# Sliding-window attention followed by SoLU and a layer norm, on one core: the division by the softmax sum is left out, and another search sets the order

## The chip, the core and the metric

One NeuronCore of a Trainium2 chip runs the whole program. Its engines work through queues of their own and meet at semaphores: PE (TensorE, matmuls; PEld is its weight load), DVE (VectorE), ACT (ScalarE), POOL (GpSimd) and SP (SyncE, which here only issues DMAs). The metric is the device time of one execution, in microseconds. The median of three runs of the kernel before is 397.25 us (396.76 to 397.73).

## The reference

Attention over a window of 31 keys and over 24 summaries of key blocks, then a two-layer network whose activation is a SoLU with a layer norm. Batch 4, 8 heads, 768 positions, 64 values a head; the network has 3072 tokens, 512 inputs and 1024 hidden values. All of it is float32.

```python
def _attn_ref(q, k, v):
    k_sum = k.reshape(B, H, nb, block, D).max(axis=3)     # block 32, nb 24
    v_sum = v.reshape(B, H, nb, block, D).mean(axis=3)
    scores_l = scale * np.matmul(q, k.transpose(0, 1, 3, 2))
    mask_l = np.abs(pos[:, None] - pos[None, :]) < window   # 16
    scores_s = scale * np.einsum('bhsd,bhnd->bhsn', q, k_sum) + np.log(block)
    scores_all = np.concatenate([np.where(mask_l, scores_l, -1e9), scores_s], axis=-1)
    ...
    a = a / (np.sum(a, axis=-1, keepdims=True) + 1e-09)
    return np.matmul(a, np.concatenate([v, v_sum], axis=2))

def _moe_ref(x, w_in, w_out, g_ln):
    h = x @ w_in
    e = np.exp(h - np.max(h, axis=-1, keepdims=True))
    sm = e / (np.sum(e, axis=-1, keepdims=True) + 1e-9)
    solu = h * sm
    mu = np.mean(solu, axis=-1, keepdims=True)
    var = np.mean((solu - mu) ** 2, axis=-1, keepdims=True)
    ln = (solu - mu) / np.sqrt(var + 1e-06) * g_ln
    return ln @ w_out
```

The layer norm takes the scale of its input out again. With Z the softmax sum, solu is u / Z for u = h * e, and (solu - mu) / sqrt(var + 1e-6) equals (u - mean(u)) / sqrt(var(u) + 1e-6 * Z * Z).

## The kernel before

The attention goes by steps: a batch, a group of four 64-query blocks (three groups a batch), and half of the heads. A step makes scores (L578, tile s), masks them and takes their minima on DVE (L597), exponentiates on ACT (L605), divides by the sum (L288), turns the result over on PE (L633, tile t), copies it out (at), and multiplies it with the values (L672, tile x; vt holds a group's value windows and, in its last 24 rows, the block means). x is split into a rounded part xh and a rest xl, since float32 matmuls are made of three matmuls of rounded parts. Two steps fill the inputs of two tiles of 128 tokens.

The network goes by those 24 tiles. `first(t)` makes h in two halves of 512 (L697, 12 matmuls each), takes the maxima (L707), exponentiates with the sum kept in hz (L712), adds the two halves' sums and takes the reciprocal on DVE (L715, L718), multiplies h by the exponential and the reciprocal with the row sum kept (L720), subtracts the mean (L723; L728, L730 or L732 on POOL, DVE or ACT), squares (L735), and makes y, the inverse root, on POOL (L739 to L745: a power by -0.5 and a step of refinement). `turn(t)` turns the tile over (lt) and splits it into lh and ll (L760); `second(t)`, four tiles behind, multiplies with w_out (L775, tile o) and scales by y on the way out (L780, os). A tile's h halves lie in PSUM banks that a later tile's h waits for (three banks for the first three tiles, then two), so L720 is also what frees a bank.

The two weight matrices come in 16 pieces of 128x1024 words. Each is rebuilt and rounded in several passes (L368 to L402, tiles raw, cv, w) on ACT, DVE and POOL, before the first matmul that reads it. `LOADS` lists the order of the first loads on SP: w a piece of w_in, k a pair of heads' keys, q queries, r rows of values for the block means of the first batch (L447, tile st_v), v value windows; capitals are the next group's.

The order is not written by hand. Every operation goes into `Plan.op` with the engines that can do it, a cost in us, and what it reads and writes. `Plan.order` plays the program: each engine takes the ready operation that can start first, and among equals that with the lowest due number. `Plan.issue` did this 64 times with noise of 3.0 on the due numbers, each time on the original numbers, and kept the order whose last matmul ended first. `keep_up` fills PE's expected pauses up to 80 us with matmuls on zeros (L900, "fillers"), which are part of the program: once queued, they are done. The plan counts a DMA's landing as 0.6 us behind its transfer up to 50 us and as 2.0 behind that.

The means of the first two batches are made on PE from loaded rows (L459, and L472 for the second batch); a DMA copies them into the last rows of each group's vt (L541, "vt<-vsum"). Those of the first batch's groups after the first went through ACT's queue, all later ones through SP's. The second batch's means go through ACT and four small DMAs on its queue (L483, L485).

## Time and profile before

| | before |
|---|---|
| median of 3 runs | 397.25 us |
| the profiled execution | 397.45 us, of which the span is 395.7 |
| PE busy, matmul instructions recorded | 386.6 us, 3697 |
| DVE, ACT, POOL busy | 275.4, 248.7, 97.9 us |
| fillers (L900), weight loads recorded | 83 |
| HBM read, written | 40.11 MB, 6.29 MB |

The page gives the busy time of each engine over the whole span, the queries give it for stretches of the span, and the rows of the timeline give single instructions with their start, their length, and in brackets how long the engine stood idle ahead of them and what ended that. A few per cent of the matmul records are missing, so counts from the order of the program are used where a count matters. The granted clock was 1.00 in every stretch up to the last matmul.

### The profile page before, as it was taken

The numbers are of one execution on the slowest core, as the hardware profiler recorded it, in microseconds if no ns is written. First come the engines' busy times: TensorE is split into PE (matmuls) and PEld (weight loads), VectorE is DVE, ScalarE is ACT, GpSimd is POOL, SyncE is SP. The second block draws the span as 40 slices with busy tenths as digits, with TensorE's granted clock in tenths as the row PEclk, the third lists the DMA queues.
The fourth block names the chain that finished last, engine by engine and source line by source line (L and its number), as shares of the span: only waits on it lengthen the run. The fifth ranks groups of instructions, "written<-read, shape, count | busy, mean of one in ns | idle before, by whom it ended". The sixth has DMA issues, their size and how long they took to land.

```text
span 395.7 us, 9677 instructions
## 1 busy us (share of the span) xinstructions
PE 386.6 (98%) x3697; PEld 298.3 (75%) x3703; DVE 275.4 (70%) x884; ACT 248.7 (63%) x746; POOL 97.9 (25%) x245
## 2 busy tenths in 40 slices
PE   8999998999999999999999999999999999999996
PEld 3436766677878888878888888878888887878776
DVE  4999998999789866577767657657657654554330
ACT  3889686999798756658558466468466463533411
POOL 4224010416837221236220121221021021101100
PEclk9999999999999999999999999999999999999999
DMA  7999992136277320463330410430310000000011
GB/s 287 411 410 369 409 329 78 56 113 185 70 248 208 113 103 0 141 175 104 123 112 2 150 66 27 156 73 28 108 48 27 2 28 27 16 12 28 27 55 53
DMA packets 14994, 49.24 MB, mean 124 GB/s; under 512 B 1836, under 2 KB 2092, under 8 KB 13412
## 3 DMA queue, kind: packets, MB, share of 16 engines
q1 hardware_dynamic: 11084, 41.89, 30.8%
q10 hardware_dynamic: 3864, 6.74, 4.7%
q8 instruction: 29, 0.48, 0.5%
q14 instruction: 17, 0.14, 0.1%
HBM read 40.11 MB, written 6.29 MB: 117 GB/s over the span
## 4 chain that ended last, share of the span: by engine, by line
PE 85%; DMA 6%; ACT 3%; DVE 2%; issue 1%; ACTq 1%; SPq 1%; DVEq 0%
PE o L775 35%; PE h L697 30%; PE x L672 6%; PE s L578 5%; PE t L633 3%; PE lt L633 3%; DMA st_v<-in_vr 3%; DMA raw<-in_w_in 2%; DMA vt<-vsum 2%; PE vs_ps L459 1%; PE x L900 1%; ACT he L712 1%; DVE he L720 1%; ACT at L281 1%; PE x L664 1%
## 5 line engine op out<-in xcount | busy, mean ns | idle before, releaser
L775 PE MATMUL o<-w,lh 128*128 128x512 f32 (+1 forms) x400 | 128.0, 390 | 0.1
L697 PE MATMUL h<-w,xh 128*128 128x512 f32 x384 | 127.0, 398 | 0.4 <-DVE he L720 0.4
L605 ACT ACTIVATE e<-e,nm 128x120 f32<-128x120 f32 x192 | 73.1, 385 | 25.0 <-DVE nm L597 25.0
L775 PEld LDWEIGHTS o<-w,lh 128*128 128x128 f32 x400 | 74.1, 188 | 18.5 <-issue 2.4
L697 PEld LDWEIGHTS h<-w,xh 128*128 128x128 f32 x384 | 72.1, 188 | 18.9 <-ACT e L605 0.8
L775 PE MATMUL o<-w,ll 128*128 128x512 f32 (+1 forms) x200 | 76.9, 384 | 0.0
L697 PE MATMUL h<-w,xl 128*128 128x512 f32 x192 | 75.6, 394 | 0.0
L707 DVE TENSOR_REDUCE hm<-h 128x1 f32<-128x512 f32 x48 | 32.6, 686 | 42.7 <-PE h L697 42.7
L281 ACT COPY at<-t 120x512 f32<-120x512 f32 x46 | 24.8, 587 | 46.1 <-PE t L633 45.6
L775 PEld LDWEIGHTS o<-w,ll 128*128 128x128 f32 x200 | 37.6, 188 | 6.6
L697 PEld LDWEIGHTS h<-w,xl 128*128 128x128 f32 x192 | 36.1, 188 | 7.5
L597 DVE CUSTOM_DVE_ANT_0 e<-s,mask 128x120 f32<-128x120 f32 x192 | 40.6, 276 | 1.3 <-PE s L578 1.3
L712 ACT ACTIVATE he<-h,hm 128x512 f32<-128x512 f32 x48 | 32.8, 697 | 9.4 <-DVE hm L709 9.4
L605 ACT ACTIVATION_READ_ACCUMULATOR e<-e,nm 128x1 f32 x192 | 36.5, 190 | 0.0
L760 DVE TENSOR_TENSOR ll<-lt,lh 128x512 fp32r<-128x512 f32 x48 | 31.9, 682 | 6.0 <-ACT lh L281 5.8
L739 POOL TENSOR_SCALAR ss<-ss 128x1 f32<-128x1 f32 x24 | 7.1, 297 | 115.0 <-ACT sq L735 114.9
L720 DVE SCALAR_TENSOR_TENSOR he<-h,hz,he 128x512 f32<-128x512 f32 x48 | 34.1, 746 | 0.4
L672 PE MATMUL x<-at,vt 120*64 120x64 f32 (+1 forms) x768 | 28.3, 225 | 1.5 <-ACT at L281 1.5
L672 PEld LDWEIGHTS x<-at,vt 120*64 120x64 f32 (+1 forms) x768 | 24.6, 138 | 6.3 <-ACT at L281 2.8
L288 DVE TENSOR_TENSOR e<-e,z 128x960 f32<-128x960 f32 x23 | 26.6, 1156 | 0.5
L281 ACT CAST lh<-lt 128x512 fp32r<-128x512 f32 x33 | 18.6, 596 | 12.9 <-PE lt L633 10.0
L735 ACT ACTIVATE sq<-he 128x1024 bf16<-128x1024 f32 x24 | 25.2, 1050 | 0.2
(94 smaller groups left out, 499.6 us busy)
## 6 DMA issues: line engine op xcount, KB each, us to landing
vt<-in_v SPq DMA_DIRECT2D x12, 1024.0 KB, 5.4
kraw<-in_k SPq DMA_DIRECT2D x16, 400.0 KB, 9.1
out<-os ACTq DMA_DIRECT2D x23, 256.0 KB, 2.0
qt<-in_q SPq DMA_DIRECT2D x11, 512.0 KB, 5.5
raw<-in_w_in SPq DMA_DIRECT2D x8, 512.0 KB, 10.7
raw<-in_w_out SPq DMA_DIRECT2D x8, 512.0 KB, 9.5
st_v<-in_vr SPq DMA_DIRECT2D x6, 512.0 KB, 12.5
st_v<-in_vb SPq DMA_DIRECT2D x8, 384.0 KB, 3.3
```

Source lines behind the costliest of these rows:

```text
L281: by = {act: lambda: nc.scalar.copy(out=to(), in_=of()), dve: lambda: nc.vector.tensor_copy(out=to(), in_=of()), pool: lambda: nc.gpsimd.t ...
L288: by = {dve: lambda: nc.vector.tensor_tensor(out=to(), in0=a(), in1=b(), op=kind), pool: lambda: nc.gpsimd.tensor_tensor(out=to(), in0=a() ...
L597: nc.vector.tensor_tensor_reduce(out=e.ap[:, n, :], in0=sc.ap[:, j, (2 * i + up) * KC:(2 * i + up + 1) * KC], in1=mask[:, mi, :], scale=-S ...
L605: nc.scalar.activation(out=e.ap[:, n, :], in_=e.ap[:, n, :], func=AF.Exp, bias=nm.ap[:, n:n + 1], scale=-1.0, accum_out=z.ap[:, n:n + 1])
L672: nc.tensor.matmul(xp()[j * D:(j + 1) * D, i, qs], vs.ap[:k, u, cs], at.ap[:k, u % 2, n[j] + u // 2, :], start=not apart, stop=not apart o ...
L697: nc.tensor.matmul(hp.ap, a.ap[:, c, ts], w.ap[:, i], start=(c == 0 and n == 0), stop=(c == NKC - 1 and n == 2))
L707: op(dve, 0.6, lambda i=i, hp=hp: nc.vector.tensor_reduce(out=nms.ap[:, i:i + 1], in_=hp.ap, op=ALU.max, axis=AX.X, negate=True), r=[hp], ...
L712: op(act, 0.71, lambda i=i, hp=hp: nc.scalar.activation(out=part(i), in_=hp.ap, func=AF.Exp, bias=nm.ap, accum_out=zs.ap[:, i:i + 1]), r=[ ...
L720: op(dve, 0.67, lambda i=i, hp=hp: nc.vector.scalar_tensor_tensor(out=part(i), in0=hp.ap, scalar=zs.ap[:, 0:1], in1=part(i), op0=ALU.mult, ...
L735: op(act, 1.13, lambda: nc.scalar.activation(out=sq.ap, in_=e.ap, func=AF.Square, accum_out=ss.ap), r=[e], w=[sq, ss])
L760: op(dve, 0.6, lambda part=part, r=r: nc.vector.tensor_tensor(out=part(lo), in0=tp.ap[:, r], in1=part(hi).bitcast(F32), op=ALU.subtract), ...
L775: nc.tensor.matmul(o.ap[:, cols], a.ap[:, f, :], w.ap[:, i, cols], start=(f == 0 and n == 0), stop=(f == NFC - 1 and n == 2))
```

## The change

The SoLU's division is left out: L720's product has 1.0 in place of the reciprocal, and the sum and the reciprocal (L715, L718 on DVE) are gone. Three operations of one element on POOL form (Z + 1e-9), times 1e-3, squared, and L739's addition takes that in place of the constant 1e-6. In the attention one broadcast of the first batch's means (its third group's) goes through SP instead of ACT. The planner's numbers and its search are others: 800 tries with a noise of 10, the first 16 on the original numbers, later ones on the best so far with noise on 2% of the operations; each order is then replayed six times with other durations and later landings (`replay`), and the sum of the last matmul's end and half of the mean end decides. `LOADS` has another order.

```diff
-LOADS = "wwkwqkkkqwwwrrrwwvQV"
+LOADS = "wkwqkkwkqwwrwrrwwvQV"
...
-    LATE = 50.0
+    LATE = 30.0
...
-    TRIES, NOISE = 64, 3.0
+    TRIES, NOISE = 800, 10.0
+    FIRST, FEW = 16, 0.02
+    PLAYS, JITTER, LAND = 6, 0.06, 1.5
...
-        due, best = [o.due for o in self.ops], None
-        for seed in range(self.TRIES):
-            noise = random.Random(seed)
-            for o, x in zip(self.ops, due):
-                o.due = x + (noise.gauss(0.0, self.NOISE) if seed else 0.0)
+        due, best, rnd = [o.due for o in self.ops], None, random.Random(0)
+        for i in range(self.TRIES):
+            noise = [x + (rnd.gauss(0.0, self.NOISE) if i < self.FIRST or rnd.random() < self.FEW else 0.0) * (i > 0)
+                     for x in (best[3] if i >= self.FIRST else [0.0] * len(due))]
+            for o, x, n in zip(self.ops, due, noise):
+                o.due = x + n
             order = self.order()
             if order:
-                end = max(o.end for o in order if "pe" in o.can)
-                if best is None or end < best[0]:
+                end = sum(self.replay(order, random.Random(k)) for k in range(self.PLAYS))
+                if best is None or end <= best[0]:
...
+    def replay(self, order, rnd):
+        free, end, held, dma, last, total, n = {}, {}, 0.0, 0.0, 0.0, 0.0, 0
+        for o in order:
+            e = o.engine
+            t = max([free.get(e, self.START)] + [end[d] + (0.0 if d.engine == e == "pe" else self.SYNC) for d in o.deps])
+            x = o.can[e][0] * (1 if e == "pe" else 1.0 + self.JITTER * (rnd.random() - 0.2))
+            other = free.get("pool", 0.0) if e == "dve" and o.port else held if e == "pool" else 0.0
+            x = t + x * (2 if e == "pe" and t < self.COLD else 1) + max(other - t, 0.0)
+            free[e] = end[o] = x
+            if e == "dve" and o.port:
+                held = x
+            if o.nbytes:
+                dma = max(dma, x + 1.0) + o.nbytes / (self.RATE if dma > self.COLD else self.SLOW) * 1e-3
+                end[o] = dma + (0.6 if dma < self.LATE else 2.5) + rnd.expovariate(1.0) * self.LAND * (dma > self.LATE)
+            if e == "pe":
+                last, total, n = max(last, x), total + x, n + 1
+        return last + 0.5 * total / n
...
-                o.end = dma + (0.6 if dma < self.LATE else 2.0)
+                o.end = dma + (0.6 if dma < self.LATE else 2.5)
...
-        e, cost, queue = (sp, 0.43, nc.sync) if b else (act, 0.8, nc.scalar)
+        e, cost, queue = (sp, 0.43, nc.sync) if b or g > 1 else (act, 0.8, nc.scalar)
...
-        op(dve, 0.07, lambda: nc.vector.tensor_scalar(
-            out=zs.ap[:, 0:1], in0=zs.ap[:, 0:1], scalar1=zs.ap[:, 1:2], scalar2=1e-9, op0=ALU.add, op1=ALU.add),
-           w=[zs])
-        op(dve, 0.1, lambda: nc.vector.reciprocal(out=zs.ap[:, 0:1], in_=zs.ap[:, 0:1]), w=[zs])
+        op(pool, 0.3, lambda: nc.gpsimd.tensor_tensor(
+            out=zs.ap[:, 0:1], in0=zs.ap[:, 0:1], in1=zs.ap[:, 1:2], op=ALU.add), w=[zs])
+        op(pool, 0.3, lambda: nc.gpsimd.tensor_scalar(
+            out=zs.ap[:, 0:1], in0=zs.ap[:, 0:1], scalar1=1e-9, scalar2=1e-3, op0=ALU.add, op1=ALU.mult), w=[zs])
+        op(pool, 0.3, lambda: nc.gpsimd.tensor_tensor(
+            out=zs.ap[:, 0:1], in0=zs.ap[:, 0:1], in1=zs.ap[:, 0:1], op=ALU.mult), w=[zs])
         for i, hp in enumerate(hs):
             op(dve, 0.67, lambda i=i, hp=hp: nc.vector.scalar_tensor_tensor(
-                out=part(i), in0=hp.ap, scalar=zs.ap[:, 0:1], in1=part(i), op0=ALU.mult, op1=ALU.mult,
-                accum_out=ss1.ap[:, i:i + 1]), r=[hp, zs], w=[(e, i), (ss1, i)])
+                out=part(i), in0=hp.ap, scalar=1.0, in1=part(i), op0=ALU.mult, op1=ALU.mult,
+                accum_out=ss1.ap[:, i:i + 1]), r=[hp], w=[(e, i), (ss1, i)])
...
-            out=ss.ap, in0=ss.ap, scalar1=1.0 / DF, scalar2=1e-6, op0=ALU.mult, op1=ALU.add), w=[ss])
+            out=ss.ap, in0=ss.ap, scalar1=1.0 / DF, scalar2=zs.ap[:, 0:1], op0=ALU.mult, op1=ALU.add), r=[zs], w=[ss])
```

The whole order moves, and with it the lines: what was L697 is L722, L720 is L749, L541 is L566, L900 is L929. Three places of it follow; each row is a line, an operation, what it writes and what it reads. In the new order PE has 31, 15, 2, 8, 3, 5 and 4 fillers ahead of its first h matmul (before: 19, 5, 17, 12, 8, 4 and 7), with both head halves' first scores in one piece each, and 3, 1, 7 and 2 behind it (before: 1, 7 and 3).

SP, the start of its queue, up to the first rows of values that PE reads for the means (st_v_0). Before, from its first row:

```order
L356 DMA raw_93<-in_w_in 128x1024
L430 DMA kraw_0_99<-in_k 128x800
L529 DMA qt_0_101<-in_q 128x512 x2
L430 DMA kraw_0_99<-in_k 128x800
L356 DMA raw_105<-in_w_in 128x1024
L356 DMA raw_107<-in_w_in 128x1024
L356 DMA raw_109<-in_w_in 128x1024
L430 DMA kraw_1_111<-in_k 128x800 x2
L356 DMA raw_117<-in_w_in 128x1024
L356 DMA raw_119<-in_w_in 128x1024
L529 DMA qt_1_122<-in_q 128x1024
L447 DMA st_v_0_125<-in_vr 128x1024
```

After it, from the second row (the first is the same piece of w_in):

```order
L381 DMA raw_99<-in_w_in 128x1024
L455 DMA kraw_1_101<-in_k 128x800
L455 DMA kraw_0_103<-in_k 128x800
L455 DMA kraw_1_101<-in_k 128x800
L554 DMA qt_0_106<-in_q 128x512
L560 DMA vt_0_108<-in_v 128x2048
L455 DMA kraw_0_103<-in_k 128x800
L381 DMA raw_111<-in_w_in 128x1024
L554 DMA qt_0_106<-in_q 128x512
L830 DMA g_sb<-in_g_ln 128x8
L472 DMA st_v_2_118<-in_vr 128x1024
L472 DMA st_v_0_121<-in_vr 128x1024
```

The second pair of heads is now complete first, the value windows of the first group are loaded early, and fewer pieces of w_in stand ahead of the rows of values.

ACT, around the means of the second batch (vs, vsum) and up to the copies of at_2_0. Before:

```order
L541 DMA vt_2_717<-vsum_508 24x4x512
L281 CAST xh_1_735<-x_1_1_825 128x512
L605 ACTIVATE e_2_0_812,z_2_0_859<-e_2_0_812,nm_2_0_813 128x120 x8
L483 COPY vs_889<-vs_ps_853 128x512
L610 ACTIVATE z_2_0_859<-z_2_0_859 128x8
L485 DMA vsum_896<-vs_889 6x512
L281 COPY kw_0_0_869<-kraw_0_722 128x8x96
L485 DMA vsum_896<-vs_889 6x512 x3
L400 ACTIVATE w_918<-cv_779,g_sb 128x512
L732 ACTIVATE he_822<-he_822,nmu_915 128x512
L281 COPY at_2_0_944<-t_2_0_920 120x512 x2
```

After it:

```order
L630 ACTIVATE e_2_0_869,z_2_0_894<-e_2_0_869,nm_2_0_870 128x120 x8
L737 ACTIVATE he_929,hz_930<-h_0_782,hm_923 128x512
L635 ACTIVATE z_2_0_894<-z_2_0_894 128x8
L737 ACTIVATE he_929,hz_930<-h_1_830,hm_923 128x512
L508 COPY vs_946<-vs_ps_915 128x512
L393 ACTIVATE cv_955<-raw_239 128x512
L510 DMA vsum_963<-vs_946 6x512 x4
L399 ACTIVATE cv_955<-raw_239 128x512
L425 ACTIVATE w_993<-cv_819,g_sb 128x512
L306 COPY at_2_0_999<-t_2_0_974 120x512 x2
```

The broadcast into vt_2 has left the queue (on SP it stands behind the key loads of the second batch), and the means are made one tile later, with the exponentials of tile 2 ahead of them.

DVE, tile 0's product and what follows it. Before:

```order
L715 TENSOR_SCALAR hz_690<-hz_690 128x1
L718 RECIPROCAL hz_690<-hz_690 128x1
L720 SCALAR_TENSOR_TENSOR he_689,s_725<-h_0_565,hz_690,he_689 128x512
L720 SCALAR_TENSOR_TENSOR he_689,s_725<-h_1_626,hz_690,he_689 128x512
L678 TENSOR_TENSOR xl_1_743<-x_1_0_700,xh_1_735 128x512
```

After it:

```order
L313 TENSOR_TENSOR e_1_1_602<-e_1_1_602,z_1_1_636 128x960
L749 SCALAR_TENSOR_TENSOR he_686,s_721<-h_0_450,he_686 128x512
L749 SCALAR_TENSOR_TENSOR he_686,s_721<-h_1_562,he_686 128x512
L732 TENSOR_REDUCE hm_737<-h_0_621 128x1
L703 TENSOR_TENSOR xl_1_745<-x_1_0_701,xh_1_735 128x512
```

The two operations on hz are gone from the row, and the attention's division of step 1_1 stands directly ahead of the product.

5 lines of the change are left out of this document (3 added, 2 removed).

## The prediction

> **What bounds the kernel now.** I read the page's first lines, then busy time by stretches cut where the trace changes character.
>
> ```profile
> span 395.7 us, 9677 instructions
> PE 386.6 (98%) x3697; PEld 298.3 (75%) x3703; DVE 275.4 (70%) x884; ACT 248.7 (63%) x746; POOL 97.9 (25%) x245
> ...
> 0.00:38.32 38.32, 34.94 (x383) 16.90 (x388) 32.59 (x111) 28.52 (x87) 13.23 (x34) 1.00 0.97 371
> 38.32:97.00 58.68, 56.15 (x594) 40.88 (x592) 56.00 (x172) 49.78 (x141) 14.27 (x30) 1.00 0.59 198
> 97.00:392.65 295.65, 295.56 (x2726) 240.50 (x2724) 186.78 (x603) 169.93 (x520) 70.37 (x181) 1.00 0.24 79
> 392.65:395.70 3.05, 0.00 (x0) 0.00 (x0) 0.00 (x0) 0.47 (x1) 0.00 (x0) 0.87 0.13 43
> ...
> GB/s 287 411 410 369 409 329 78 56 113 185 70 248 208 113 103 0 141 175 104 123 112 2 150 66 27 156 73 28 108 48 27 2 28 27 16 12 28 27 55 53
> ...
> 0.00:100.00 100.00, 20.69 (x77) 7.92 (x83) 1.00 0.73 262
> ```
>
> Columns of a stretch: length, then busy us of PE, PEld, DVE, ACT, POOL, the granted clock, the DMA share, GB/s. From 97 us to the last matmul PE is busy for 295.56 of 295.65 us, while DVE (187) and ACT (170) have over 100 us of room; what the change saves or adds there is hidden as long as that room lasts. The last 3.05 us are one copy and the output DMA, which the change leaves. So the time can only change before 97 us: 3.4 us of waiting up to the first h matmul (38.32 less 34.94), 2.5 us from there to 97, and the fillers of L900 (matmuls on zeros that keep PE's clock up), 20.69 us for 83 weight loads (last row, that line alone; the GB/s are those of the page's 40 slices). DVE is full there: 56.00 of 58.68 us. What PE waits for, of the stretches to 40 us and from 40 to 97 us (us in total, times, longest):
>
> ```profile
> PE vs_ps L459 <- DMA st_v<-in_vr: 0.9, 1, 0.9
> ...
> PE x L672 <- ACT at L281: 1.5, 2, 1.0
> PE s L578 <- DVE ll L760: 0.4, 1, 0.4
> PE h L697 <- DVE he L720: 0.4, 1, 0.4
> ```
>
> **The change part by part.** *To the first h matmul.* PE's order has 68 fillers there instead of 72, and s_1_1's scores come behind the first h matmuls instead of ahead. PE's timeline, with one row each of ACT and DVE:
>
> ```profile
> 1.24 6.50 PE L900 MATMUL vs_ps<-zero 128*128 128x512 bf16 x19 [1.24 <-DVE zero L303]
> ...
> 11.16 3.84 PE L900 MATMUL vs_ps<-zero 128*128 128x512 bf16 x16
> 14.93 0.38 PE L578 MATMUL s<-kraw,qt 64*64 64x96 f32 x2
> ...
> 17.09 2.54 PE L900 MATMUL vs_ps<-zero 128*128 128x512 bf16 x11 [0.16 <-issue]
> 20.52 1.88 PE L459 MATMUL vs_ps<-st_v,sel 128*24 128x512 f32 x4 [0.90 <-DMA st_v<-in_vr]
> 22.33 0.69 PE L633 MATMUL t<-ident,e 64*120 64x64 f32 x16
> 22.95 1.90 PE L900 MATMUL x<-zero 128*128 128x512 bf16 x8
> 24.78 1.05 PE L578 MATMUL s<-kw,qt 64*64 64x120 f32 x32
> ...
> 26.74 3.61 PE L459 MATMUL vs_ps<-st_v,sel 128*24 128x512 f32 x8
> ...
> 31.92 0.65 PE L664 MATMUL x<-at,vsum 24*64 24x256 f32 x4
> ...
> 34.53 1.46 PE L900 MATMUL h<-zero 128*128 128x512 bf16 x6 [0.16 <-issue]
> ...
> 38.32 0.50 PE L697 MATMUL h<-w,xh 128*128 128x512 f32 x1
> ...
> 9.44 0.94 DVE L439 TENSOR_REDUCE ksum<-kraw 128x24 f32<-128x768 f32 x1
> ...
> 16.56 0.69 ACT L374 ACTIVATE cv<-raw 128x512 int32<-128x512 uint32 x1 [0.72 <-DMA raw<-in_w_in]
> ```
>
> Seventeen fillers in a row take 3.77 us (11.16 to 14.93; one record is missing), 0.22 each. The 31 that now open PE end 12 x 0.22 behind 7.7, at 10.4. The first scores then need their second key load: 2,224 KB are queued up to it, where before 1,824 KB were at the 9.44 of the DVE row. (A load is its rows by its elements, as the order shows them, by 4 bytes: 512 KB for 128x1024.) At 411 GB/s, the second of the page's 40 slices, 400 KB are 1.0 us, so with 0.94 for the maxima the scores start between 10.4 and 11.3. They take 2.0 us (14.93 to 16.93), 15 fillers 3.3 and the gap of 0.16: 15.9 to 16.8. The second score group needs 4,672 KB queued, as the w_in piece did for which ACT waited until 16.56: it starts at 16.6 to 16.8 and ends at 18.8 at the latest; two fillers, 19.2 to 19.4. The first value rows, whose landing PE waited for until 20.52, now have 5,700 KB queued instead of 6,208: 1.3 us earlier, 19.2, and that wait goes. Behind them come, each from its start to the next one's in these rows, 0.22 a filler: 1.9 (means), 1.8 (8 fillers), 0.6 (t), 0.7, 3.6 (means), 0.6, 1.1, 2.4 (x), 1.0 (s_1_0), 0.9, 2.4 (x), with 0.16 for one gap: 17.2. The first h matmul starts at 36.4 to 36.6, say 36.5, against 38.3 less the 1.0 of s_1_1 that is no longer ahead, 37.3: **-0.8**. Bounds: -1.7, if keys and queries are early and only the counted fillers hold PE, and +0.3, if the subtract that frees x_0_0's bank (x_0_1 waits for it) is a POOL pass late.
>
> *The broadcast that moves to SyncE.* That "SyncE issues more" is one transfer of 192 KB, vt_2<-vsum. Its old place in the chain of waits, and the DMA issues of ACT's queue behind it:
>
> ```profile
> 53.50 6.18 DMA vt<-vsum
> 59.69 1.35 issue
> 61.04 0.72 ACTq L485
> ...
> 65.41 0.95 ACT at L281 x2
> ...
> 97.16 5.60 PE h L697 x24
> ...
> 61.90 2.13 ACTq L485 DMA_DIRECT2D vsum<-vs x3
> ```
>
> ACT could not issue the new means (L485) before the broadcast had landed, 1.35 us of standing still, and the copies of at_2_0 behind them made PE wait 1.0 of the 1.5 us. On SP it stands behind the key loads and has landed long before the means, which PE now makes one tile later. What it can hold up on SP is the 1 MB load behind it, of which the first reader is the x behind tile 4's h matmuls, over 20 us on. But the four issues stay ahead of at_2_0 (0.72 + 2.13 us), and PE has only 18 h matmuls between the means and x instead of 27, so it arrives 9 x 0.23 = 2.1 us sooner (24 take 5.60, as in the chain) while ACT saves 1.35. I take a wait of 0.7 for 1.0: **-0.3**, with 0 and 1.8 us of wait as bounds (-1.0, +0.8). The Trainium skill ("DMA: Bandwidth & Descriptors", Issuing engines are not separate DMA queues) says that another issuing engine saves only the issue. By it the 6.18 us would stay and this term would be 0; the 1.35 us of the chain's row are ACT's wait for a landing, which that rule does not price.
>
> *Fillers after the first h matmul:* 13 instead of 11, 2 x 0.22: **+0.4**.
>
> *The SoLU.* Per tile two DVE operations go:
>
> ```profile
> 47.29 0.21 DVE L715 TENSOR_SCALAR hz<-hz 128x1 f32<-128x1 f32 x1
> 47.54 0.16 DVE L718 RECIPROCAL hz<-hz 128x1 f32<-128x1 f32 x1
> 47.82 0.75 DVE L720 SCALAR_TENSOR_TENSOR he<-h,hz,he 128x512 f32<-128x512 f32 x1
> ...
> L739 POOL TENSOR_SCALAR ss<-ss 128x1 f32<-128x1 f32 x24 | 7.1, 297 | 115.0 <-ACT sq L735 114.9
> ...
> L745 POOL TENSOR_SCALAR ss<-ss 128x1 f32<-128x1 f32 x24 | 4.6, 190 | 1.7
> ```
>
> From the exponentials' sum to the product it was 0.53 us (47.29 to 47.82), and h's bank is free that much sooner. The one wait for it, 0.4 us, goes: **-0.4** (0 if the next h half is held by another engine). With an immediate for the pointer the product itself I keep at 0.75 (bounds 0.65 and 0.85). POOL gets three operations of one element: 24 x 3 x 0.19 to 0.3 us, 14 to 22 us of an engine that is 25% busy; they end under ACT's square, which needs the centred tile first. The variance's operation keeps its count. After 97 us both cost nothing, and without that cover a tile's 0.6 to 0.9 us on POOL would have to outlast four tiles of delay before L780 reads y.
>
> *POOL's part in splitting the weights.* Before 97 us POOL makes 8 wide adds and subtracts, up from 5. What such a pass does to DVE:
>
> ```profile
> 20.05 1.71 POOL L289 TENSOR_TENSOR cv<-cv 128x512 int32<-128x512 int32 x1
> ...
> 20.57 1.75 DVE L379 SCALAR_TENSOR_TENSOR cv<-cv 128x512 int32<-128x512 int32 x1
> ...
> 30.07 0.68 DVE L379 SCALAR_TENSOR_TENSOR cv<-cv 128x512 int32<-128x512 int32 x1
> ```
>
> Beside POOL's pass the same DVE operation took 1.75 instead of 0.68 us. A pass can cost DVE 0 to 1.07 us, three more 0 to 3.2, against 3 x 0.7 that DVE no longer does itself. I take **+0.2**. The Trainium skill ("SBUF — State Buffer", Who interferes with whom) says that the two engines lock a shared pair of ports for a whole instruction, whoever starts first. The rows agree, and by it the price is paid only where the passes meet.
>
> Sum: -0.8 - 0.3 + 0.4 - 0.4 + 0.2 = -0.9. The profiled execution took 397.45 us (span 395.7 and 1.75 around it), so 396.55; the median of the runs, 397.25, lies 0.2 lower, and on it the forecast is **396.4 us**.
>
> **Rivals.** *The waits go altogether.* With the 2.5 us behind the first h matmul gone too, only fillers are left: -0.8 - 2.5 + 0.4 = -2.9, and at the first term's lower bound -3.8. For it: the search now replays each order six times with other durations and later landings. Against it: the order has new tight places, x_2_1 right behind at_2_1. New waits of half that size leave -1.65 and the median at 395.6.
>
> *The waits move.* DVE and ACT are full (56.00 and 49.78 of 58.68 us), and an order takes little work away: 5 tiles x 2 small operations. Then the 0.8 of the start is given back at x_2_0, x_2_1 and tile 4's h: 397.2.
>
> *POOL holds DVE.* At the bound of 1.07 us, two of the three passes in front of what PE waits for next (x_0_0's subtract behind w_484's pass, the w_out pieces ahead of tile 0's o) give +2.1 in place of +0.2, so 397.25 - 0.9 + 1.9 = 398.3. It decides from one pass (1.07 us) on; against it: in the trace only two of five passes lengthened a DVE operation.
>
> That the change fails to do what it says leaves only the order: the removed operations do not return.
>
> **How the numbers follow.** Forecast (395.9 to 397.0) 0.40; waits gone (395.9 and below) 0.19; waits moved (396.9 to 397.9) 0.26; POOL holds DVE (over 397.9) 0.15. About 0.2%, 0.8 us, is what a measurement of this kernel can tell from no change: 396.46 to 398.04. The second case and 0.25 of the first lie below, so faster 0.44; the rest of the first and nearly all of the third within, 0.40; slower 0.16. The range leaves out some 0.1 at either end: 394.9 to 398.4.
>
> **What would show it.** In the new profile: the first h matmul at 36.5; no wait of vs_ps for st_v; x for at at 0.7 us; no wait of h for he; PE still busy without a break from about 96 us. Wrong would make it a first h matmul behind 37.3, DVE operations of over 1 us at L404 beside POOL's L314, or a wait of PE anywhere after 100 us.

## The result, and the profile after

The kernel got slower: median 400.53 us (400.40 to 401.46) against 397.34 (396.76 to 397.73) for the kernel before on the same chip, a ratio of 1.0089 with an interval of 1.0076 to 1.0103. Forecast were 396.4 and a range of 394.9 to 398.4. The profiled execution took 400.42 us, of which the span is 398.7; before, the span was 395.7, so the records hold 3.0 of the 3.2 us.

The first lines of the page of the changed kernel:

```profile
span 398.7 us, 9720 instructions
...
PE 388.0 (97%) x3701; PEld 296.6 (74%) x3701; DVE 258.4 (65%) x818; ACT 255.0 (64%) x754; POOL 121.3 (30%) x327
...
L742 POOL TENSOR_TENSOR hz<-hz 128x1 f32<-128x1 f32 x24 | 4.7, 196 | 106.0 <-ACT he L737 106.0
```

and its busy time by stretches, cut as before at the first h matmul, at 97 us and at the last matmul (length, then PE, PEld, DVE, ACT, POOL, clock, DMA share, GB/s):

```profile
0.00:36.93 36.93, 32.81 (x352) 15.14 (x353) 29.04 (x79) 23.89 (x63) 11.36 (x32) 1.00 0.96 366
36.93:97.00 60.07, 57.38 (x625) 40.87 (x621) 58.35 (x177) 52.33 (x158) 23.12 (x50) 1.00 0.54 190
97.00:395.62 298.62, 297.81 (x2734) 240.63 (x2730) 170.97 (x564) 178.35 (x534) 86.86 (x246) 1.00 0.25 81
```

DVE did lose work (275.4 to 258.4 us in all) and the first h matmul does start earlier (36.93). The surprise is the last line. The clock is 1.00 and PE is as good as full, in both kernels. But up to its last matmul the stretch is longer than before's, 298.62 against 295.65 us, though PE has the same work left within a few matmuls.

Stretches of time hide that, because the two kernels stand at different places in their work at 97 us. So I cut both traces by work: each matmul counts with its usual step, fillers not at all, and a row of this table ends when both have started the same amount.

| nominal matmul work | before: us (idle, fillers) | after: us (idle, fillers) | change |
|---|---|---|---|
| 0 to 12 us | 36.97 (2.14, 17.63) | 36.72 (2.88, 17.86) | -0.25 |
| 12 to 20 | 9.02 (0, 0) | 9.07 (0, 0) | +0.05 |
| 20 to 30 | 11.61 (0, 0) | 12.88 (0.57, 0.93) | +1.27 |
| 30 to 40 | 13.19 (1.37, 0) | 11.91 (0, 0) | -1.28 |
| 40 to 50 | 14.17 (0.50, 2.53) | 15.22 (1.71, 1.89) | +1.05 |
| 50 to 60 | 12.51 (0.66, 0) | 12.64 (0.42, 0) | +0.13 |
| 60 to 344, from 97 or 98 us on | 294.75 (0.06, 0) | 296.77 (0.79, 0) | **+2.02** |

Up to the seventh row the sum is +1.0, where -0.9 was forecast. The other 2.0 us are lost where nothing was to happen; 0.7 of them are small new gaps, and 1.3 are matmuls that follow each other more slowly. The single rows depend on the steps that are taken for the small matmuls: with other averages they shift by up to 1.5 us, while the first six together stay at +1.0 to +1.1 and the last row at +1.9 to +2.0. So only these two sums are used.

What PE waits for in the changed kernel, of the stretches to 40 us, 40 to 97, and 97 on (us in total, times, longest):

```profile
PE s L603 <- DMA qt<-in_q: 2.1, 2, 1.8
PE vs_ps L484 <- DMA st_v<-in_vr: 0.7, 1, 0.7
...
PE s L603 <- DVE ll L789: 1.5, 1, 1.5
PE h L722 <- DVE xl L703: 0.6, 1, 0.6
PE t L658 <- DVE e L313: 0.4, 1, 0.4
PE o L804 <- DVE w L427: 0.2, 1, 0.2
...
PE h L722 <- DVE he L749: 0.4, 2, 0.2
PE vs_ps L541 <- DVE ll L789: 0.3, 1, 0.3
```

The wait of x for at (1.5 us before) is gone. In its place stand s for ll (1.5) and h for xl (0.6). Both can be followed back. First ACT and DVE ahead of ll, from their timelines (start, length, in brackets idle time and what ended it):

```profile
66.48 2.83 ACTq L510 DMA_DIRECT2D vsum<-vs  x4
69.35 0.68 ACT L399 ACTIVATE cv<-raw 128x512 int32<-128x512 uint32 x1 [2.33 <-DMA vsum<-vs]
...
72.55 1.05 ACT L306 CAST lh<-lt 128x512 fp32r<-128x512 f32 x2
...
73.63 1.29 DVE L789 TENSOR_TENSOR ll<-lt,lh 128x512 fp32r<-128x512 f32 x2 [0.47 <-ACT lh L306]
```

ACT issues the four small copies of the second batch's means (L510) and computes nothing for 2.33 us. It has no gap after that until lh, on which ll and then PE's scores wait. Second, DVE and POOL ahead of xl:

```profile
52.97 0.68 DVE L404 SCALAR_TENSOR_TENSOR cv<-cv 128x512 int32<-128x512 int32 x1
...
56.19 1.82 DVE L404 SCALAR_TENSOR_TENSOR cv<-cv 128x512 int32<-128x512 int32 x1
57.94 0.68 DVE L703 TENSOR_TENSOR xl<-x,xh 128x512 fp32r<-128x512 f32 x1
...
56.18 1.28 POOL L314 TENSOR_TENSOR cv<-cv 128x512 int32<-128x512 int32 x1
```

One weight pass on DVE took 1.82 instead of 0.68 us, beside an add on POOL that began 10 ns earlier; xl is queued right behind it.

### The profile page after: what moved, and what is told of

The parts are those of the page before. It is cut to its first block, busy times and chain, and to the rows that moved or that the text cites. A ratio compares the mean times of both kernels' runs of the same rounds, so it can differ in the third digit from the quotient of the medians.

```text
span 398.7 us, 9720 instructions
## 1 busy us (share of the span) xinstructions
PE 388.0 (97%) x3701; PEld 296.6 (74%) x3701; DVE 258.4 (65%) x818; ACT 255.0 (64%) x754; POOL 121.3 (30%) x327
## 4 chain that ended last, share of the span: by engine, by line
PE 74%; DMA 10%; DVE 9%; ACT 4%; ACTq 1%; SPq 0%; issue 0%
PE o L804 33%; PE h L722 28%; DMA vt<-in_v 5%; PE x L697 4%; PE s L603 3%; PE t L658 3%; PE lt L658 3%; DMA st_v<-in_vr 2%; DMA kraw<-in_k 2%; DVE he L749 1%; DVE e L622 1%; DVE cv L404 1%; ACT at L306 1%; ACT e L630 1%; DVE cv L408 1%; DVE e L313 1%
## 5 line engine op out<-in xcount | busy, mean ns | idle before, releaser
L722 PE MATMUL h<-w,xh 128*128 128x512 f32 x384 | 132.9, 402 | 0.4 <-DVE he L749 0.4
L804 PE MATMUL o<-w,lh 128*128 128x512 f32 (+1 forms) x400 | 130.6, 389 | 0.2 <-DVE w L427 0.2
L722 PEld LDWEIGHTS h<-w,xh 128*128 128x128 f32 x384 | 72.1, 188 | 21.3 <-issue 2.8
L722 PE MATMUL h<-w,xl 128*128 128x512 f32 x192 | 76.0, 396 | 0.6 <-DVE xl L703 0.6
L809 ACT ACTIVATE os<-o,y 128x512 f32<-128x512 f32 (+1 forms) x23 | 15.4, 670 | 44.4 <-PE o L804 44.4
L722 PEld LDWEIGHTS h<-w,xl 128*128 128x128 f32 x192 | 36.1, 188 | 8.8 <-DVE xl L703 1.5
L749 DVE SCALAR_TENSOR_TENSOR he<-h,he 128x512 f32<-128x512 f32 x48 | 32.4, 689 | 14.1 <-ACT he L737 14.1
L306 ACT COPY at<-t 120x512 f32<-120x512 f32 x42 | 22.9, 585 | 23.1 <-PE t L658 19.9
L742 POOL TENSOR_TENSOR hz<-hz 128x1 f32<-128x1 f32 x24 | 4.7, 196 | 106.0 <-ACT he L737 106.0
L697 PE MATMUL x<-at,vt 120*64 120x64 f32 (+1 forms) x768 | 28.1, 225 | 0.0
L697 PEld LDWEIGHTS x<-at,vt 120*64 120x64 f32 (+1 forms) x768 | 24.5, 138 | 4.6 <-issue 2.7
L306 ACT CAST lh<-lt 128x512 fp32r<-128x512 f32 x38 | 21.2, 602 | 9.0 <-PE o L804 6.2
L757 POOL TENSOR_SCALAR he<-he,nmu 128x512 f32<-128x512 f32 x17 | 17.4, 1027 | 29.6 <-DVE nmu L752 29.6
```

The lines of the kernel that those rows point to most:

```text
L306: by = {act: lambda: nc.scalar.copy(out=to(), in_=of()), dve: lambda: nc.vector.tensor_copy(out=to(), in_=of()), pool: lambda: nc.gpsimd.t ...
L697: nc.tensor.matmul(xp()[j * D:(j + 1) * D, i, qs], vs.ap[:k, u, cs], at.ap[:k, u % 2, n[j] + u // 2, :], start=not apart, stop=not apart o ...
L722: nc.tensor.matmul(hp.ap, a.ap[:, c, ts], w.ap[:, i], start=(c == 0 and n == 0), stop=(c == NKC - 1 and n == 2))
L749: op(dve, 0.67, lambda i=i, hp=hp: nc.vector.scalar_tensor_tensor(out=part(i), in0=hp.ap, scalar=1.0, in1=part(i), op0=ALU.mult, op1=ALU.mult,
L757: op(pool, 0.62, lambda sl=sl: nc.gpsimd.tensor_scalar(out=e.ap[:, sl], in0=e.ap[:, sl], scalar1=nmu.ap, scalar2=1.0, op0=ALU.add, op1=ALU ...
L804: nc.tensor.matmul(o.ap[:, cols], a.ap[:, f, :], w.ap[:, i, cols], start=(f == 0 and n == 0), stop=(f == NFC - 1 and n == 2))
```

## The experiments

In all kernels but the seventh the order is a list written into the kernel (operation, engine, fillers) in place of the search; with the lists of the two kernels it gives their instructions. So the SoLU can be changed without another order, and an order without another SoLU. "Step" is the mean time from the start of one h or o matmul to the next inside a run of them, between 100 and 368 us: 230.75 ns before, 232.42 after, over 820 to 860 steps. Times are medians with their range, ratios are against the kernel before on the same chip. The experiments ran on several chips; the kernel before has medians of 397.1 to 397.3 on them, so a difference of two medians across chips is good to some tenths of a us. In the expectations, A holds the order to be the cause (A1 by the mixing of runs, A3 by the places of the tiles), C the copies on ACT's queue, H the pass of POOL, and F says that fillers only fill waits.

### Which part: the SoLU or the order

e1 is the kernel before with the new SoLU, its order kept:

```diff
-        op(dve, 0.07, lambda: nc.vector.tensor_scalar(
...
-        op(dve, 0.1, lambda: nc.vector.reciprocal(out=zs.ap[:, 0:1], in_=zs.ap[:, 0:1]), w=[zs])
+        op(pool, 0.3, lambda: nc.gpsimd.tensor_tensor(
...
-                out=part(i), in0=hp.ap, scalar=zs.ap[:, 0:1], in1=part(i), op0=ALU.mult, op1=ALU.mult,
+                out=part(i), in0=hp.ap, scalar=1.0, in1=part(i), op0=ALU.mult, op1=ALU.mult,
```

> The order of the kernel before, held fixed instruction by instruction on every engine, with only the SoLU changed: 2 VectorE instructions of a tile replaced by 3 of GpSimd at the same place, the product's scalar 1.0, the epsilon from the squared sum. Theory A (the loss sits in the new order, not in the SoLU): 396.9 us (396.5 to 397.4), that is the before's time less at most its 0.4 us wait of h for the product; the mean step of the h and o matmuls inside a run (start to start, under 260 ns, 100 to 368 us) stays at the 230.8 ns of the profile of before. Theory B (GpSimd's 72 more instructions, or the epsilon that waits for GpSimd, cost the 3 us): 399 to 400.5 us, the step near the 232.4 ns of the changed kernel.

396.67 us (395.81 to 397.26), ratio 0.9989 (0.9979 to 0.9999), step 230.75. The wait of h for he is gone. So the SoLU alone is worth some -0.45 us here (the interval of the ratio ends just short of 1), and it loses nothing with the old order. The loss comes with the new one. e2 is the other half, the new order with the old SoLU, the diff above the other way round:

> The order of the changed kernel, held fixed, with the old SoLU put back: 2 VectorE instructions ahead of a tile's first product in place of the 3 of GpSimd. Theory A (the loss sits in the order): 400.5 to 401.5 us, step 232.4 ns, a little longer than the changed kernel since VectorE gets 48 instructions back in a busy start. Theory B (GpSimd's instructions): 397.5 to 398.5 us, step near 230.8 ns.

415.2 us, ratio 1.0462 (1.0445 to 1.0478): a miss, and no clean undo. Its list of waits opens with

```profile
PE h L698 <- DVE he L722: 10.0, 12, 1.4
```

The new order was made for a product that waits for no sum, and the old product is late in it tile after tile. The step, though, is 232.45 with this SoLU too: it belongs to the order.

### What slows the matmuls: the mixing of the runs?

The new order mixes the h and o matmuls of a tile in runs of 3 to 24, mostly under 20; most runs of the old one are of 24. e3 takes the changed kernel and sorts 21 stretches of PE's list into all o, then all h; e4 takes the kernel before and mixes 15 tiles by threes. One place of e3's list (the rows of PE alone; 573 to 576 are pieces of three o matmuls of a tile, 527 to 533 pieces of three h matmuls):

```diff
-507p 515p 527p 528p 529p 573p 532p 510p 533p 574p 575p 576p
+507p 515p 573p 527p 528p 529p 532p 510p 574p 575p 576p 577p
```

> The changed kernel with its order held fixed, but in 21 stretches between two small pieces from about 110 us on TensorE does first all groups of o and then all of h, as the kernel before does, in place of pieces of 3 to 21 in turn; the start and the other engines' orders are the changed kernel's. Theory A1 (the step of the matmuls follows how often h and o change places): step 231.0 ns or less in place of 232.4, 1.2 to 1.8 us less, 398.9 to 399.4 us. Theory A2 (the step has another cause): 232.4 ns, 400.5 us, or more where waits come in.

> The kernel before with its order held fixed, but in 15 tiles from about 110 us on TensorE mixes o and h: 12 matmuls of o, then h and o in turn by 3, then 12 of h, in place of 24 of o and 24 of h (some 130 more changes between the two). Theory A1 (the step follows the changes): 232.4 ns or more, 398.7 us or more. Theory A2: 230.8 ns, 397.3 us, plus whatever waits the mixing brings, which the trace names.

e3: 428.19 us, ratio 1.0789 (1.0767 to 1.0812), and a step of 232.54, not the 230.75 of before. e4: 406.57, ratio 1.0246 (1.0232 to 1.026), step 231.46. Both became slow by waits (in e3 t waits for e 6.3 us in all, in e4 h for he 3.8; in e3 the granted clock also fell four times): the queues of the other engines had been left as they were. But long runs didn't bring the faster step back, so the mixing isn't what makes the difference between the two kernels. In e4 the step did rise by 0.7 ns, to between the numbers of the two theories (230.8 and 232.4); what mixing does by itself these two runs don't settle.

### What slows the matmuls: the places of the tiles

What else differs is where the tiles lie in SBUF. The pool gives a place to each tile at its first use in the order, so another order moves them: in the built programs the buffers xh, xl, lh, ll (the stationary operands of h and o) have other addresses, while the weights, the moving operand, lie in both at 19552 plus multiples of 4096. e5 is the changed kernel, same instructions and order, with the tiles in the places of the kernel before; e6 is e1 with the places of the changed kernel:

```diff
+PLACE = "raw0 raw2 raw3 ... y5 y6"
...
+        for x in PLACE.split():
+            self.first[x].ap
```

> The changed kernel, instruction by instruction and wait by wait, with nothing else changed than where its tiles lie in SBUF: every buffer gets the address that it has in the kernel before (the pool hands out addresses in the order of first use, so the new order had moved them). Theory A3 (the step of the h and o matmuls depends on where their operands lie): step 230.8 ns in place of 232.4, about 1,060 steps by 1.6 ns = 1.7 us less, 398.5 to 399.1 us. Theory A4 (the step follows the order or what the other engines do meanwhile): 232.4 ns, 400.5 us.

> The first experiment's kernel (the order of before, the new SoLU; 396.7 us, step 230.8 ns) with every buffer at the address that it has in the changed kernel, nothing else changed. Theory A3: step 232.4 ns, 1.7 us more, 398.2 to 398.8 us. Theory A4: 230.8 ns, 396.7 us.

e5: 399.01 us (398.1 to 400.4), ratio 1.0046 (1.0025 to 1.0067), step 231.06. e6: 397.94 (397.41 to 398.7), ratio 1.0013 (0.9994 to 1.0032), step 232.48. So the places carry +1.3 us (e6 against e1) to +1.5 (changed kernel against e5); by the ratios it is +1.0 and +1.7. The order at equal places leaves the step within 0.3 ns (231.06 for 230.75, 232.48 for 232.42). In the row of the table from 97 us on e5 takes 295.66 us, with the same 0.79 idle as the changed kernel, which takes 296.77. The chain of waits shows it in pieces that count a run's matmuls (start, us, what); first the changed kernel, then e5:

```profile
228.56 4.17 PE o L804 x18
234.83 2.80 PE h L722 x12
```

```profile
229.02 4.10 PE o L793 x18
235.19 2.75 PE h L711 x12
```

The same matmuls, on an engine that waits for nothing, take 232 and 228 ns each (4.17 and 4.10 by 18), and 233 and 229 (2.80 and 2.75 by 12).

e7 measures the rule by itself. No other engine works while PE multiplies; the whole computation is left out, and groups of 24 pairs of weight load and matmul (f32r, 128x128 by 128x512) run with the stationary tile at every 32nd byte of 512 and the moving one at five places:

```diff
+    for c, (hi, lo, mov) in enumerate(configs()):
...
+                nc.tensor.matmul(o, at(a + 512 * f, P), at(w + 2048 * i, 512), start=f == 0 and n == 0, stop=f == 7 and n == 2)
```

> No attention and no SoLU: only 103 groups of 24 matmuls of 128x128 by 128x512 in the order of passes of the kernel (high piece by low weights, low by high, high by high), with the stationary and the moving operand at addresses that are varied from group to group, and no other engine at work; the output is a constant. Theory A3, addresses alone: the mean step differs between the groups by up to 6 ns (227 to 233), and the four pairs of addresses of before and the pairs of after give the steps that the kernels show (227.6 for the pair 127328 and 143456, 233.3 for 186016 and 190112). If addresses matter only by collisions with what the other engines read and write: one step for all groups.

It ran once. The mean step of a group behind its first five steps, by stationary less moving address, modulo 256, with both stationary tiles of a pair (high and low part) at the same difference:

| difference | step, ns |
|---|---|
| 0 | 226.7 to 227.8 |
| 192 (64 bytes below) | 228.9 |
| 96 | 234.1 to 234.4 |
| all others tried (every 32) | 232.8 to 233.4 |

Sixteen pairs of places at an equal remainder, each 4096 bytes on, all took 226.7. Left out is the first group, 326.8, which began at a lower granted clock. The kernels' own addresses in the same run give their steps: 233.3 for xh_0 and xl_0 of both kernels (233.3 to 233.4 in the kernels), 228.9 for xh_1 and xl_1 of the one before (229.2 to 229.9), 226.7 for its lh_1 and ll_1 (228.1), 233.3 for lh_0 and ll_0 of the changed one (233.2). Three pairs have their two tiles at unequal differences, and two of these fit the kernels less well: lh_0 and ll_0 of the kernel before (64 and 0) take 231.1 alone and 232.4 in the kernel, lh_1 and ll_1 of the changed one (64 and 192) 231.8 and 231.9, its xh_1 and xl_1 (192 and 224) 233.3 and 231.7. Why the step depends on this difference no run shows.

If the rule holds, the kernel before can be made faster, and slower, by nothing but addresses. e9 is e1 with the eight stationary buffers given out first, at the remainder of the weights (lh and ll lie in the buffers that first hold the rows for the means, st_v); e17 is e9 with one small tile of 32 bytes ahead of them:

```diff
+PLACE = "raw0 ... raw14 st_v0_0 st_v0_1 st_v0_2 st_v1_0 xh0_0 xh0_1 xl0_0 xl0_1 sel kraw0_0 ..."
...
-PLACE = "... raw14 st_v0_0 st_v0_1 ..."
+PLACE = "... raw14 nm0_0_0 st_v0_0 st_v0_1 ..."
```

> The first experiment's kernel (order of before, new SoLU, 396.7 us) with nothing changed but addresses: the eight buffers of the stationary operands (xh, xl, lh, ll, two each) lie first in the pool, at 85088 and 4096 bytes on each, so that they agree with the weights (19552 and on) in the address modulo 256. From the matmuls alone: 226.7 ns a step where both agree modulo 256, 228.9 where the stationary one is 64 bytes below, 231 to 234 elsewhere. Theory A3 as a rule: step 226.7 to 227.2 ns in place of 230.8, some 1,130 steps by 4 ns = 4.6 us less, 392.1 us (391.6 to 392.7). If the rule doesn't hold beside other engines: 395.5 to 397 us.

> The aligned kernel of the order of before (new SoLU, 393.1 us) with its eight buffers moved up by 32 bytes, to 85120 and on, nothing else changed. Theory A3 as a rule (the step depends on the difference of the two operands' addresses modulo 256): the matmuls alone showed 233.3 ns at a difference of 32, so 233.3 ns a step in place of 226.7 to 228, some 1,130 steps by 6 ns = 6.5 us more, 399 to 400 us; that would be slower than any layout of this order so far. If it was only the place at the pool's start that helped: 393.1 us.

e9: 393.06 us (392.44 to 393.48), ratio 0.9899 (0.9885 to 0.9914), step 227.41. e17: 398.82 (397.99 to 399.55), ratio 1.0037 (1.0024 to 1.005), step 233.21. Thirty-two bytes are worth 5.8 us (5.5 by the ratios). Runs of 24 in the chains of the kernel before, of e9 and of e17:

```profile
209.33 5.75 PE o L775 x24
215.08 5.60 PE h L697 x24
...
223.86 5.66 PE o L775 x24
229.52 5.49 PE h L697 x24
```

```profile
206.44 5.67 PE o L790 x24
212.10 5.44 PE h L709 x24
...
220.72 5.67 PE o L790 x24
226.38 5.44 PE h L709 x24
```

```profile
209.86 5.79 PE o L790 x24
215.65 5.60 PE h L709 x24
...
224.43 5.79 PE o L790 x24
230.21 5.60 PE h L709 x24
```

Before, a run took 5.60 or 5.49 us as its buffer fell well or badly; all h runs here take 5.44 in e9 and 5.60 in e17. Each o run here follows smaller matmuls: its first step takes some 337 ns in all three kernels, and the next few 230 to 236 in e9 too, so alignment gains less there. That is part of why e9 came out 1.0 us above the 392.1 expected, 0.4 outside its range; the rest is not taken apart. The same edit on the changed kernel, e11:

> The changed kernel (400.5 us), every instruction and wait as it is, with the same eight buffers at the same aligned addresses as in the two runs of the order of before. Theory A3 as a rule: step 226.7 to 227.2 ns in place of 232.4, some 1,130 steps by 5.6 ns = 6.3 us less, 394.2 us (393.6 to 394.8). What is left above the aligned order of before is then the price of the new order alone, without its addresses: by the traces 0.96 us behind at the end of the start plus some 0.4 us of waits and changes after it, 1.0 to 2.2 us. If the order has no price of its own, both come out within 0.5 us of each other.

396.23 us (395.5 to 397.39), ratio 0.9979 (0.9968 to 0.9989), step 227.57: 4.3 less than the changed kernel, where 6.3 was expected, in part for the same reason. Against e9 the new order is still 3.2 us slower, though the steps are now alike (227.57 and 227.41): the rest of its loss isn't in the matmuls.

### The rest of the order's loss: two waits and the fillers

e8 has the four small copies of the second batch's means on SP, not ACT:

```diff
-            op(act, 0.34, lambda g=g: nc.scalar.dma_start(
+            op(sp, 0.43, lambda g=g: nc.sync.dma_start(
```

> The changed kernel with its order held fixed, but the four row transfers of the means (vsum from vs, 2.83 us of issuing on ScalarE from 66.5 us) go out from SyncE, which issues nothing from 56 to 70 us. Theory C (in the start ScalarE's queue is what TensorE waits for at 73.7 us, through at, sq, lh and ll): the wait of s for ll of 1.5 us goes, h after it starts up to 1.5 us earlier, and since TensorE is busy from there on the whole 1.0 to 1.5 us arrive at the end: 399.0 to 399.5 us. Theory D (VectorE, busy without a gap from 73.6 to 78.3 us, sets h there): under 0.5 us, 400.1 to 400.5 us.

399.72 us (399.48 to 401.5), ratio 1.0068 (1.0046 to 1.009). From its list of waits:

```profile
PE s L580 <- POOL kw L285: 0.6, 1, 0.6
PE h L699 <- DVE xl L680: 0.6, 1, 0.6
```

The wait for ll is gone and a smaller one, for the keys, has come up from behind it. By itself the gain of 0.8 is within the scatter; the same edit on the aligned kernels is clear. e10 is e9 with it, e12 is e11 with it:

> The kernel of the run beside it (order of before, new SoLU, aligned buffers) with the four row transfers of the means issued by SyncE in place of ScalarE, whose 2.9 us of issuing stand ahead of the copy at that x waits for by 1.0 us at 66 us. Theory C (ScalarE's queue sets the start there too): 0.5 to 1.1 us less than the run beside it. Theory D (something else is late next): 0 to 0.3 us less.

> The run beside it (the changed kernel, aligned) with the row transfers of the means issued by SyncE: as between the changed kernel and its run with the rows by SyncE, 0.6 to 1.0 us less.

e10: 391.87 us (391.64 to 392.08), ratio 0.9871 (0.9858 to 0.9883), 1.2 below e9. e12: 394.86 (394.57 to 395.21), ratio 0.9948 (0.9935 to 0.996), 1.4 below e11. The second is more than the 0.6 to 1.0 expected. The order before paid for these copies too, though which wait the time came out of its traces don't show: x waits 0.5 us for at in e9 and in e10 alike. e10 beats both kernels.

e14 puts the add that met DVE's pass onto DVE, behind xl; e16 sends the broadcast through ACT again:

```diff
-... 247p 243d 305d 228o 259p ...
+... 247p 243d 228d 305d 259p ...
...
-        e, cost, queue = (sp, 0.43, nc.sync) if b or g > 1 else (act, 0.8, nc.scalar)
+        e, cost, queue = (sp, 0.43, nc.sync) if b else (act, 0.8, nc.scalar)
```

> The changed kernel with its order held fixed, but one wide GpSimd pass (the add of the weights' conversion at 56.2 us, 128x512, 1.28 us) goes to VectorE, right behind the xl for which h waits 0.57 us at 58.1 us. Theory H (the pass holds VectorE's operation beside it, 1.82 us in place of 0.68): that operation takes 0.7 us, xl comes 1.1 us earlier, the wait of 0.57 us goes and arrives at the end: 399.8 to 400.2 us. Theory I (something else is late next there): the wait stays or moves, 400.3 to 400.7 us.

> The changed kernel with its order held fixed, but the broadcast of the means into the third group's values (at 52.9 us) is issued by ScalarE again, as in the kernel before, in place of SyncE. Theory J (the move to SyncE helps by about what the forecast gave it): 0.2 to 0.9 us more, 400.7 to 401.4 us. Theory K (it changes nothing, ScalarE has slack there): 400.3 to 400.7 us. Were the move a part of the loss: less than 400.2 us.

e14: 399.81 us (399.42 to 400.75), ratio 1.0072 (1.0059 to 1.0084), and no wait for xl. e16: 399.62 (399.29 to 401.19), ratio 1.0076 (1.0058 to 1.0095), and no wait for xl either, which wasn't expected of it. Its timelines of DVE and POOL at that place tell why:

```profile
55.95 0.69 DVE L381 SCALAR_TENSOR_TENSOR cv<-cv 128x512 int32<-128x512 int32 x1
...
55.98 1.80 POOL L291 TENSOR_TENSOR cv<-cv 128x512 int32<-128x512 int32 x1
```

Here DVE began 30 ns ahead of POOL, kept its 0.69, and POOL's add took 1.80. In the changed kernel POOL began 10 ns ahead, and DVE paid. By what was expected, a time under 400.2 would have made the move to SyncE a part of the loss. The run can't carry that: its interval overlaps the changed kernel's, and the 0.6 us of the wait for xl went for another reason. What it does show is that x has no wait for at here either, with the broadcast back on ACT's queue. Its whole list of PE's waits from 40 to 97 us:

```profile
PE s L580 <- DVE ll L766: 1.5, 1, 1.5
PE t L635 <- DVE e L290: 0.4, 1, 0.4
PE o L781 <- DVE w L404: 0.2, 1, 0.2
```

e13 drops the 13 fillers behind the first h matmul of the changed kernel, e15 the 11 of e10:

```diff
-... 137s x2 x2 x2 183p ... 255s s8 261p ... 294d x5 x5 x5 x5 x5 x5 x5 h9 h9 391p ...
+... 137s 183p ... 255s 261p ... 294d 391p ...
```

> The changed kernel with its order held fixed, without the 13 dummy matmuls that stand behind the first h (4 between 47 and 56 us, 9 ahead of an h at 78 us). Theory F (they only fill time in which TensorE would wait): the same time within 0.4 us, 400.1 to 400.9 us, the waits longer by what the dummies took (0.9 and 1.9 us). Theory G (they stand in the way): 0.9 us less from the first 4, up to 2.8 us less in all, 397.7 to 399.6 us.

> The fastest kernel so far (order of before, new SoLU, aligned buffers, the means' rows by SyncE: 391.9 us) without its 11 dummy matmuls behind the first h, 2.4 us of TensorE between 69 and 83 us. Theory F: 391.5 to 392.3 us. Theory G: 389.5 to 391 us.

e13: 400.51 us (400.07 to 401.4), ratio 1.0086 (1.0073 to 1.0099), no change; PE's idle time grew instead. e15: 393.18 (391.76 to 393.62), ratio 0.9895 (0.988 to 0.9911), 1.3 us above e10 (1.0 by the ratios) and outside both theories. These fillers stand in for waits and are no cost of their own; they also keep the clock up. The stretch of e13 in which the changed kernel has a clock of 1.00:

```profile
37.00:97.00 60.00, 55.88 (x618) 40.92 (x615) 58.36 (x178) 52.48 (x159) 23.02 (x50) 0.97 0.55 189
```

In this execution h waits 1.59 us for he where nine fillers stood, and behind that the granted clock is 0.5 for 3.4 us. PE is 1.3 us late by 82 us and has caught up by 91, mostly where the changed kernel waits for w and e. The mean clock of all five runs of e13 is 0.991 to 0.996, where three of the changed kernel's four have 0.999 or 1.000. In e15 the loss seems to reach the end: its one run with a clock of 0.999 took 391.76, like e10, and its four with 0.994 to 0.996 took 393.07 to 393.62.

e18 puts the repairs together: the changed kernel aligned, its copies on SP, the add on DVE.

> The changed kernel with three repairs at once: aligned buffers, the means' rows by SyncE (these two together 394.9 us), and the add of 56.2 us on VectorE (0.7 us alone). If the parts add: 394.1 us (393.7 to 394.5), still 1.8 to 2.6 us behind the order of before with the same aligned buffers and rows (391.9 us). If the start's parts hide one another: 394.6 to 395.1 us.

394.35 us (394.12 to 394.64), ratio 0.9929 (0.9917 to 0.9941): the parts add up, and it is 6.2 below the changed kernel. It is still 2.5 behind e10 (2.3 by the ratios). In the profiled executions, 3.0 apart, the cut by work puts 2.0 of it before 97 us and 1.0 after (0.66 of that idle). They are several small waits; no run takes them apart, and this stays open.

## Why the prediction was wrong, point by point

**The step that failed is the first one**: "PE is busy for 295.56 of 295.65 us ... what the change saves or adds there is hidden ... So the time can only change before 97 us". The room of the other engines was there. But busy is a share of time, not an amount of work: a full engine can still take longer for the same matmuls, and it did, by 2.0 us. The places of the stationary tiles carry 1.1 to 1.3 of them (the row from 97 us on in e5 and e6), small gaps 0.7 (0.79 idle against 0.06, the same in e5, e11 and e18). The order decides both the queues and, through the tile pool, the addresses; the prediction read only the queues. No rival contained this, though "a wait of PE anywhere after 100 us" and a DVE operation of over 1 us at L404, two of its own signs of being wrong, both came.

**The sum before 97 us** came out at +1.0 instead of -0.9.

- *To the first h matmul, -0.8.* The first h starts at 36.93; against the 37.3 of before that is -0.4, half the size and inside the bounds. PE's timeline has two of the steps otherwise:

```profile
17.00 0.42 PE L603 MATMUL s<-kraw,qt 64*64 64x96 f32 x8 [1.83 <-DMA qt<-in_q]
...
19.64 1.88 PE L484 MATMUL vs_ps<-st_v,sel 128*24 128x512 f32 x4 [0.72 <-DMA st_v<-in_vr]
...
36.93 0.50 PE L722 MATMUL h<-w,xh 128*128 128x512 f32 x1
```

  The second scores wait 1.83 us for queries, longer than the loads ahead of them let me expect (17.00 for 16.6 to 16.8), and the wait of vs_ps for st_v, which was to go, is 0.72.
- *The broadcast, -0.3.* x no longer waits for at at all, better than the 0.7 forecast (whose own terms, 1.0 and 2.1 less 1.35, give 1.75). But the move didn't do it: e16, with the broadcast on ACT's queue again, has no such wait either. Which part of the new order took it away no run shows. And what is late next was looked for in the wrong place. The four issues were priced (2.85 us on ACT) against at_2_0 only; they now stand ahead of lh, and s waits 1.5 us for ll, where it was 0.4. e8 took that wait away. "The waits move" was the right rival for this, at the wrong price.
- *Fillers, +0.4.* Wrong in kind: e13 without them took the same time. They fill waits, and one of these waits lowers the clock when they are gone.
- *The SoLU, -0.4.* Right in e1, which gained 0.45 and has no wait of h for he. In the changed kernel two such waits of 0.2 stand behind 97 us, against "no wait of h for he". The product got cheaper too (0.69 for 0.75).
- *POOL's passes, +0.2.* The mechanism was right and the size wrong. One pass held DVE by 1.1 us (1.82 for 0.68) at a place where xl is next, which e14 puts at 0.7. "POOL holds DVE", given 0.15, named this part of the loss; it said that one pass decides, and one pass was 0.7 of the 3.2 us.

The Trainium skill ("SBUF — State Buffer", Who interferes with whom) was cited for the lock of the shared ports, whoever starts first; the pair of the changed kernel and e16 agrees, with the price on the engine that starts second, 1.82 on DVE or 1.80 on POOL. By the Trainium skill's rule on issuing engines ("DMA: Bandwidth & Descriptors", Issuing engines are not separate DMA queues) another engine saves only the time of the issue. For the four copies that time was ACT's 2.33 us of standing still, and moving them gained 1.2 and 1.4 us (e10, e12).

Put together, of +3.2 us: the SoLU -0.45; the places +1.3 (e6 less e1) to +1.5 (changed less e5), by the ratios +1.0 and +1.7; the order at equal places +2.3 (e5 less e1) to +3.2 (e11 less e9), of which the copies on ACT's queue 0.8 (e8) and the pass of POOL 0.7 (e14), each with ranges that overlap those of the changed kernel, and the rest open.

## What to carry to other kernels

When an order, a pool or a tag changes, compare the addresses of the matmul operands as well as the queues, and judge a full engine by its step between like instructions, not by its busy share. Here float32 matmuls were fastest with the stationary tile at the remainder of the moving one modulo 256, and giving those tiles out first was worth 3.6 us (e9 against e1), eight times the SoLU's 0.45. When a wait is removed from an engine's queue, price everything that now stands behind the same slow instructions, not only the next in line.

## What the hardware showed that was not expected

- The step of back-to-back f32r pairs depends on the difference of operand addresses modulo 256: 226.7, 228.9, 233.3 or 234.1 ns with the other engines at rest (e7), and within 1.6 ns of e7's steps in the kernels. It is no matter of the clock, granted at 1.00 in e7 behind its first group and from 97 us on in the kernels compared (e3, whose clock fell, aside).
- In the two meetings of a DVE and a POOL pass shown above, the one that started second paid, and 10 to 30 ns decided over 1.1 us of DVE's time.
- After a wait of 2.17 us the granted clock was down for some us. PE's timeline in e3, the same x without a wait ahead of it and after one, and then the stretches' busy time and clock:

```profile
112.42 1.15 PE L674 MATMUL x<-at,vt 120*64 120x64 f32 x32
...
125.40 0.69 PE L635 MATMUL t<-ident,e 64*120 64x64 f32 x16 [2.17 <-DVE e L290]
...
126.60 1.97 PE L674 MATMUL x<-at,vt 120*64 120x64 f32 x32
```

```profile
110.00:123.00 13.00, 12.37 (x144) 9.54 (x136) 8.39 (x39) 10.05 (x41) 6.51 (x16) 1.00 0.88 277
...
126.00:131.00 5.00, 5.00 (x87) 4.49 (x84) 3.83 (x14) 4.54 (x8) 2.56 (x8) 0.66 0.06 13
```

  The clock was 1.00 before it and, as the mean of the last stretch, 0.66 behind it: 0.5 for 3.4 us, then 1.00 again. The length of the wait alone doesn't decide it: e13's clock fell behind 1.59 us and e5's behind 1.97, while the changed kernel kept 1.00 behind 1.83 and e2 behind 2.09. Of the changed kernel's four runs the longest, 401.46, is the one with a mean clock of 0.996; the others have 0.999 or 1.000.
